# Strassen's scheme for layer 1 of the last two of four batches, in a fused attention and MLP kernel

## The chip, the cores and the metric

One core of a Trainium2 chip runs the whole program. The metric is device time in microseconds of one execution; a run's time is compared as the median of several.

## The reference

For each of 4 batches and 8 heads (768 positions, 64 features) a query sees a local window (keys less than 16 positions away) and 24 block summaries (the maximum of each 32 keys, the mean of each 32 values, with log 32 added to the score). The heads' outputs are joined to x, 3072 tokens of 512 features, and go through two layers:

```python
    a = np.exp(scores_all)
    a = a / (np.sum(a, axis=-1, keepdims=True) + 1e-09)
    v_all = np.concatenate([v, v_sum], axis=2)
    return np.matmul(a, v_all).astype(np.float32)
...
    h = x @ w_in
    g = np.maximum(0.01 * h, h)
    return (g @ w_out).astype(np.float32)
```

w_in is 512 x 2048, w_out 2048 x 512, all in fp32.

## The kernel before

**Split operands.** Both layers run in fp32r. Each operand is kept as a high part (rounded to fp32r) and a low part (what is left, in fp32r too), and a product is three matmuls: high x high, high x low, low x high. The weights are loaded raw, one 512 KB load per feature tile and layer, and split by `weights` (lines 613 to 651): ScalarE makes the high part (line 641), VectorE the low one (line 644). The parts stay in `win_hi`, `win_lo`, `wout_hi` and `wout_lo` for the whole run.

**Chunks.** The tokens go in 8 chunks of 384 (`T`), two to a batch. Chunk c has its x in one of two buffers, as 4 blocks of 128 features (`xh`, `xl`). `mlp` (line 665) works a chunk in 16 feature tiles of 128. `m1` is 12 matmuls (4 blocks of features, three products, 384 columns, line 676) into one of two PSUM banks `h`. ScalarE applies the leaky ReLU twice, to fp32r (`ghi`, line 683) and to fp32 (`gs`, line 680), and VectorE takes the difference (`glo`, line 686). `m2` is 9 matmuls of 512 columns (lines 695 to 697): three token blocks, three products, added over all 16 feature tiles into the three banks a0, a1, a2. TensorE's order is m1 of tile f, m2 of f-1, m1 of f+1, and so on. At a chunk's end the three banks are emptied by ScalarE, VectorE, ScalarE (`fin`, lines 708 and 710) and stored.

**Attention.** A unit is two heads by 128 queries, 12 units to a chunk, 96 in all. From chunk 2 on they run in quads of four: a burst of scores, transposes and products with the values is put between two MLP stages on TensorE; VectorE and ScalarE do the softmax. The values' product of a quad is copied into `xh` (line 563) and its rest into `xl` (line 566).

**The order.** `Plan` gives every operation an engine, a cost and a due time (`prio`), and simulates the engines: each takes, of what is ready, the one due first. The kernel is written out in the order that comes out, engine by engine; at run time each engine keeps to it and waits on semaphores. Due times are in units: one unit is an attention unit's share of a chunk, a chunk is 12 units, and the MLP begins at `LEAD` = 15.54. `PLACE` maps the attention units of a chunk to due times. Buffers are rings: an operation that allocates the k-th use of a tag waits for all users of the use before it. All loads and stores are issued by SyncE, in one queue. Raw weights, keys and block values share six buffers of 512 KB, `big`.

Of the kernel before, what the change touches and what calls it, by code (L numbers as in the profile page):

```python
# [8 lines left out]
F32 = mybir.dt.float32  # L9
# [28 lines left out]
PARTS = [(0, 0, SPL), (1, 0, NF), (0, SPL, NF)] + [(c, 0, NF) for c in range(2, NCH)]  # L38
XB = [0, 1] + [(c + 1) % 2 for c in range(2, NCH)]
PLACE = {0: (0.0, 1.0), 1: (13.07, 0.61), 2: (22.42, 0.495), 3: (36.92, 0.51)}  # L40
# [11 lines left out]
B1 = 6  # L52
USQ = 1.424
# [9 lines left out]
class Plan:  # L63
# [5 lines left out]
    def __init__(self):  # L69
        self.ops, self.rings, self.users = [], {}, {}  # L70
# [11 lines left out]
    def join(self, o, prio, after=(), use=(), alloc=()):  # L82
# [4 lines left out]
        for key in use:  # L87
            self.users.setdefault(key, []).append(o)

# [61 lines left out]
def build(tc, ctx, a):  # L151
# [5 lines left out]
    ps_acc, ps_h, ps_s, ps_t = psum("pacc", 1), psum("ph", 2), psum("pss", 1), psum("pst", 1)  # L157

    win_hi = cst.tile([128, 4, DF], F32R, name="win_hi")
    win_lo = cst.tile([128, 4, DF], F32R, name="win_lo")  # L160
# [10 lines left out]
    for i, (x, n) in enumerate(((xh, XGAP[0]), (xh, XGAP[1]), (xl, XGAP[2]), (xl, XGAP[3]))):  # L171
        gap(n, cst, f"x{i}")
        x.append(cst.tile([128, NP, T], F32R, name=f"x{i}"))
# [14 lines left out]

    mask_op = load_op(("mask",), -8.7, lambda: nc.sync.dma_start(out=mask, in_=a["mask"]), size=128 * (3 * LK + 44) * 4)
# [10 lines left out]
    def k_max(b, p, t, ahead):  # L200
        def load():
            x = new("big", ("kn", b * CPB, p), [128, 1024], bufs=BIG)
# [6 lines left out]
        kn_op[key] = load_op(key, t - 1.3 - ahead, load, after=gate(b), alloc=[("big", key, BIG)], size=128 * (S + 2 * WIN) * 4)  # L209
# [4 lines left out]
    def v_mean(b, j, t, ahead):  # L214
        def load():
            x = new("big", ("vb", b, j), [128, 1024], bufs=BIG)
# [10 lines left out]
        o = load_op(("vb", b, j), t - 1.0 - ahead, load, after=gate(b), alloc=[("big", ("vb", b, j), BIG)], size=96 * 4096)  # L227
# [6 lines left out]
    def v_mean_pe(t):  # L234
        def load(j):
            x = new("big", ("vb", 0, j), [128, 1024], bufs=BIG)
# [13 lines left out]
        for j in range(3):  # L250
            o = load_op(("vb", 0, j), t - 4.5 + 0.1 * j, lambda j=j: load(j), alloc=[("big", ("vb", 0, j), BIG)], size=128 * 4096)
# [6 lines left out]
    def operands(c, p, t, ahead):  # L258
# [5 lines left out]
        def load_k():  # L264
            x = new("big", kw, [128, 1024], bufs=BIG)
# [26 lines left out]
        if cb:  # L292
            kn_op[kw] = load_op(kw, t - 1.3 - ahead, load_k, alloc=[("big", kw, BIG)], size=128 * (T + 2 * WIN) * 4)
# [61 lines left out]
    def x_of(x, c, r, n):  # L355
        return x[XB[c]].rearrange("p a t -> p (a t)")[:, 128 * r:128 * r + n]
# [485 lines left out]
```

## Time and profile before

| | |
|---|---|
| median of 3 runs | 640.75 us (640.72 to 641.19) |
| span of the profiled execution, first to last instruction | 639.2 us |
| matmuls | 4592 |
| TensorE, busy | 633.7 us (99%) |
| VectorE, busy | 263.4 us (41%) |
| ScalarE, busy | 293.2 us (46%) |
| moved by DMA | 58.07 MB, mean 91 GB/s |
| granted TensorE clock, mean | 0.999 of 2.4 GHz |

The profiled execution has no time of its own beside its span; the runs' median is 1.55 us more than that. Matmuls overlap, so the time that one costs is the distance between two starts and not its duration.

### The profile page before, as it was taken

The numbers are of one execution on the slowest core, as the hardware profiler recorded it, in microseconds if no ns is written. First come the engines' busy times: TensorE is split into PE (matmuls) and PEld (weight loads), VectorE is DVE, ScalarE is ACT, GpSimd is POOL, SyncE is SP. The second block draws the span as 40 slices with busy tenths as digits, with TensorE's granted clock in tenths as the row PEclk, the third lists the DMA queues.
The fourth block names the chain that finished last, engine by engine and source line by source line (L and its number), as shares of the span: only waits on it lengthen the run. The fifth ranks groups of instructions, "written<-read, shape, count | busy, mean of one in ns | idle before, by whom it ended". The sixth has DMA issues, their size and how long they took to land.

```text
span 639.2 us, 11599 instructions
## 1 busy us (share of the span) xinstructions
PE 633.7 (99%) x4592; PEld 557.6 (87%) x4592; DVE 263.4 (41%) x881; ACT 293.2 (46%) x876; POOL 4.4 (1%) x10
## 2 busy tenths in 40 slices
PE   9999999999999999999999999999999999999997
PEld 7688888898888998888888888888898898989996
DVE  5899999512485213323533243132332422121111
ACT  5899985624655224435345254243543532222221
POOL 0200000000000000000000000000000000000000
PEclk9999999999999999999999999999999999999999
DMA  8897997200754100304332121111101200010001
GB/s 272 275 303 240 295 296 219 75 4 26 199 157 126 40 2 14 122 24 125 87 86 72 42 68 33 47 63 32 41 13 47 86 1 1 1 50 0 1 1 50
DMA packets 27206, 58.07 MB, mean 91 GB/s; under 512 B 3024, under 2 KB 13328, under 8 KB 27152
## 3 DMA queue, kind: packets, MB, share of 16 engines
q1 hardware_dynamic: 27152, 57.33, 29.3%
q8 instruction: 36, 0.59, 0.4%
q14 instruction: 18, 0.15, 0.1%
HBM read 48.97 MB, written 6.29 MB: 86 GB/s over the span
## 4 chain that ended last, share of the span: by engine, by line
PE 99%; ACT 0%; issue 0%; DVE 0%
PE h L676 42%; PE a L695 14%; PE a L697 14%; PE a L696 14%; PE spare L788 2%; PE vps L243 1%; PE t L346 1%; PE o L352 1%; PE s L329 1%; PE s_('B', 21)_5358 L352 0%; PE s_('B', 8)_2162 L352 0%; PE s_('B', 24)_6023 L352 0%; PE s_('B', 23)_5837 L352 0%; PE s_('B', 20)_5118 L352 0%; PE s_('B', 19)_4871 L352 0%; PE s_('B', 18)_4629 L352 0%
## 5 line engine op out<-in xcount | busy, mean ns | idle before, releaser
L676 PE MATMUL h<-x,win_hi 128*128 128x384 f32 x1024 | 262.8, 337 | 0.0
L686 DVE TENSOR_TENSOR glo<-gs,ghi 128x384 fp32r<-128x384 f32 x128 | 71.3, 557 | 304.5 <-ACT gs L680 304.2
L676 PEld LDWEIGHTS h<-x,win_hi 128*128 128x128 f32 x1024 | 185.8, 188 | 9.1 <-issue 0.2
L683 ACT ACTIVATE ghi<-h 128x384 fp32r<-128x384 f32 x128 | 62.8, 490 | 279.1 <-PE h L676 279.1
L676 PE MATMUL h<-x,win_lo 128*128 128x384 f32 x512 | 172.2, 336 | 0.0
L695 PE MATMUL a<-wout_hi,ghi 128*128 128x512 f32 x384 | 153.2, 399 | 0.0
L697 PE MATMUL a<-wout_hi,glo 128*128 128x512 f32 x384 | 151.1, 394 | 0.0
L696 PE MATMUL a<-wout_lo,ghi 128*128 128x512 f32 x384 | 150.2, 391 | 0.0
L676 PEld LDWEIGHTS h<-x,win_lo 128*128 128x128 f32 x512 | 96.1, 188 | 0.0
L697 PEld LDWEIGHTS a<-wout_hi,glo 128*128 128x128 f32 x384 | 72.1, 188 | 16.9 <-DVE glo L686 0.3
L696 PEld LDWEIGHTS a<-wout_lo,ghi 128*128 128x128 f32 x384 | 72.2, 188 | 11.3 <-DVE wout_lo L644 0.3
L695 PEld LDWEIGHTS a<-wout_hi,ghi 128*128 128x128 f32 x384 | 72.2, 188 | 10.5
L341 ACT ACTIVATE e<-e,m 128x120 f32<-128x120 f32 x192 | 73.4, 387 | 3.5 <-DVE m L334 3.5
L680 ACT ACTIVATE gs<-h 128x384 f32<-128x384 f32 x128 | 62.2, 486 | 0.0
L341 ACT ACTIVATION_READ_ACCUMULATOR e<-e,m 128x1 f32 x192 | 36.6, 191 | 0.0
L274 ACT COPY k<-kn 128x288 f32<-128x288 f32 x64 | 24.5, 432 | 5.9 <-DMA kn<-in_k_dram 5.9
L583 DVE TENSOR_TENSOR e<-e,z 128x480 f32<-128x480 f32 x36 | 23.6, 657 | 1.0
L638 DVE SCALAR_TENSOR_TENSOR raw<-raw 128x512 int32<-128x512 int32 x32 | 21.7, 689 | 0.7 <-ACT raw L635 0.3
L635 ACT ACTIVATE raw<-raw 128x512 f32<-128x512 f32 x32 | 21.4, 696 | 0.1
L207 DVE TENSOR_REDUCE ksum<-kn 128x24 f32<-128x768 f32 x16 | 15.1, 946 | 9.6 <-DMA kn<-in_k_dram 9.6
L334 DVE DVE_READ_ACCUMULATOR2_ANT m<- 128x1 f32 x192 | 15.9, 83 | 0.0
L223 DVE TENSOR_REDUCE vsum<-vb 96x32 f32<-96x1024 f32 x12 | 14.4, 1206 | 2.1 <-DMA vb<-in_vb_dram 2.1
(410 smaller groups left out, 455.8 us busy)
## 6 DMA issues: line engine op xcount, KB each, us to landing
raw<-in_w_dram SPq DMA_DIRECT2D x32, 512.0 KB
v<-in_v_dram SPq DMA_DIRECT2D x32, 288.0 KB
kn<-in_k_dram SPq DMA_DIRECT2D x16, 400.0 KB
k<-in_q_dram SPq DMA_DIRECT2D x32, 192.0 KB
out_dram<-out SPq DMA_DIRECT2D x21, 256.0 KB
vb<-in_vb_dram SPq DMA_DIRECT2D x12, 384.0 KB
kn<-in_k_dram SPq DMA_DIRECT2D x16, 208.0 KB
v<-vsum SPq DMA_DIRECT2D x24, 72.0 KB
```

The lines of the kernel that those rows point to most:

```text
L274: nc.scalar.copy(k, x)
L341: nc.scalar.activation(out=e[:, n], in_=e[:, n], func=AF.Exp, scale=-1.0, bias=m[:, n:n + 1], accum_out=z[:, n:n + 1])
L583: nc.vector.tensor_tensor(out=e, in0=e, in1=z.unsqueeze(2).broadcast_to([128, 4, LK]), op=ALU.mult)
L635: nc.scalar.activation(out=hw(), in_=hw(), func=AF.Prelu, scale=2.0 ** -112, alpha=2.0 ** 32)
L638: nc.vector.scalar_tensor_tensor(out=li(), in0=hi_i(), scalar=3, in1=li(), op0=ALU.logical_shift_left, op1=ALU.bitwise_or)
L676: nc.tensor.matmul(h[:, :T], w[:, k, 128 * f:128 * f + 128], x[:, k], start=n == 0, stop=n == 11)
L680: nc.scalar.activation(out=new("gs", G("gs", f), [128, T], bufs=1), in_=tl[G("h", f)][:, :T], func=AF.Prelu, alpha=0.01)
L683: nc.scalar.activation(out=gnew("ghi", G("ghi", f)), in_=tl[G("h", f)][:, :T], func=AF.Prelu, alpha=0.01)
L686: nc.vector.tensor_tensor(out=gnew("glo", G("glo", f)), in0=tl[G("gs", f)], in1=tl[G("ghi", f)].bitcast(F32), op=ALU.subtract)
L695: nc.tensor.matmul(o, gh, wout_hi[:, f], start=f == f0, stop=False)
L696: nc.tensor.matmul(o, gh, wout_lo[:, f], start=False, stop=False)
L697: nc.tensor.matmul(o, gl, wout_hi[:, f], start=False, stop=f == f1 - 1)
```

## The change

Chunks 0 to 3 stay as they were. For batches 2 and 3 both chunks of a batch go through layer 1 together:

- x of the batch is seen as four blocks: features in two halves, tokens in two halves (the two chunks). w_in of a pair of feature tiles is seen as four blocks too: features in two halves, the two tiles. Seven products of sums of blocks take the place of eight products (Winograd's form of Strassen's scheme). Each product is 6 matmuls of 384 columns: two 128-feature blocks, three parts.
- `prepare` (once per pair of tiles, in chunks 1 and 2) makes four weight sums and splits them, and writes these and the three plain blocks that are needed to HBM: 7 x 256 KB per pair, by six DMAs. Both batches read them back, product by product, into a ring of eight slots, six of them in a former x buffer.
- `take` copies attention's output of batches 2 and 3 to fp32 pieces in the old `big` slots 3 to 5, and `convert` makes the sums of x and splits them into the space of `win_hi` and `win_lo` (the last one in the other former x buffer).
- `product` runs the seven products of a pair on four banks: X for 1 and 2, Y for 6, W for 7 and 4, Z for 5 and 3. VectorE adds what crosses between banks (U2, U3, C22, C21, C12). The results go through the leaky ReLU and the split into `g`.
- Layer 2 comes after each two pairs (`GF` = 4 feature tiles): for each of six blocks of 128 tokens two halves of 6 matmuls into one bank, h1 or a0, and `flush` adds the bank to a sum in SBUF. The last group's blocks are stored one by one.
- `big` is six buffers until due time 23.1 and then three. Attention of chunks 3 to 5 is due earlier.

The core of the diff:

```diff
-PARTS = [(0, 0, SPL), (1, 0, NF), (0, SPL, NF)] + [(c, 0, NF) for c in range(2, NCH)]
-PLACE = {0: (0.0, 1.0), 1: (13.07, 0.61), 2: (22.42, 0.495), 3: (36.92, 0.51)}
+PARTS = [(0, 0, SPL), (1, 0, NF), (0, SPL, NF), (2, 0, NF), (3, 0, NF)]
+PLACE = {0: (0.0, 1.0), 1: (13.07, 0.61), 2: (22.42, 0.495), 3: (33, 0.8), 4: (43.2, 0.6), 5: (50.4, 0.7)}
+PLACE.update({c: (59.84 + UPC * (c - 6), 1.0) for c in range(6, NCH)})
+LATE = 23.1
+RS = 8
+GF = 4
+L1W = 2.8
+AHEAD = 2.5
...
+    NJ = NF // 2
+    ORDER = ("1", "6", "7", "5", "2", "4", "3")
+    PIECES = ((0, 1), (1, 2), (3, 4), (4, 5))
...
+        wa = w_op[2 * j, 0] + w_op[2 * j + 1, 0] + w_op[NF - 1, 1]
...
+                ks[n, l] = P.op("SP", 550, t + 0.02 * (2 * n + l), lambda n=n, w=w, l=l: keep(w, n, l), after=wa, size=128 * (2 - n) * 1024)
+        o = fw = P.op("DVE", DVE(1024), t, lambda: nc.vector.tensor_tensor(out=F, in0=win_hi[:, own].bitcast(F32), in1=win_lo[:, own].bitcast(F32), op=ALU.add),
...
+        for n, x in enumerate(((3, 2, 3, ALU.add), (2, 0, 2, ALU.subtract), (0, 3, 0, ALU.subtract), (1, 1, 0, ALU.subtract))):
+            o = P.op("DVE", DVE(256), t + 0.05 + 0.01 * n, lambda x=x: mix(*x), after=[o], use=[kf])
+        h = P.op("ACT", ACT(1024), t + 0.1, lambda: nc.scalar.copy(hi, F), after=[o], use=[kf], alloc=[("big4", kh, 1)])
...
+        c1 = split("1", full(0))
+        t3 = [mix(2, 3, 2, ALU.subtract, full(2, 3))]
+        t2 = [mix(0, 2, 0, ALU.add, t3 + c1)]
+        c6 = split("6", t2)
+        c7 = split("7", t3)
+        t4 = [mix(2, 1, 0, ALU.subtract, full(1) + t2 + c7)]
+        t1 = [mix(0, 3, 0, ALU.subtract, c6 + t4)]
+        split("5", t1)
+        split("2", full(1))
+        split("4", t4)
+        split("3", full(3))
...
+                for k in range(2):
+                    for l, y in ((0, 0), (0, 1), (1, 0)):
+                        nc.tensor.matmul(o[:, :T], w[:, 256 * l + 128 * k:256 * l + 128 * k + 128], x[y][:, T * k:T * k + T],
+                                         start=start and n == 0, stop=n == 5, skip_group_check=True)
...
+                    elif q == "6":
+                        u2 = [add("U2", "Y", "P1", True, d, [o] + c1)]
+                    elif q == "7":
+                        u3 = [add("U3", "W", "U2", True, d, [o] + u2)]
+                        hold["W"] = [o] + u3
+                    elif q == "5":
+                        c22 = [add("U3", "Z", "U3", False, d, [o] + u3)]
+                        hold["Z"] = [o] + c22
+                        gate_out(2 * j + 1, 1, "U3", c22, d + 0.6)
+                    elif q == "2":
+                        gate_out(2 * j, 0, "X", [o], d + 0.1)
+                    elif q == "4":
+                        c21 = [add("P1", "W", "U2", False, d, [o] + u3)]
+                        gate_out(2 * j + 1, 0, "P1", c21, d + 0.1)
+                    elif q == "3":
+                        c12 = [add("U2", "Z", "U2", False, d, [o] + c22 + c21)]
+                        gate_out(2 * j, 1, "U2", c12, d + 0.3)
...
+            parts = [(0, 0, 0), (0, 1, 0), (0, 0, 1), (0, 1, 1), (0, 2, 0), (0, 2, 1)] + [(1, i, s) for i in range(TPC) for s in range(2)]
...
+                    for f in (GF * n + 2 * s, GF * n + 2 * s + 1):
+                        gh, gl = (y[:, 128 * i:128 * i + 128] for y in g_of(f, h))
+                        for g, w in ((gh, wout_hi), (gh, wout_lo), (gl, wout_hi)):
+                            nc.tensor.matmul(o, g, w[:, f], start=s + m == 0, stop=s == 1 and m == 5)
...
+    for j in range(NF // 2):
+        prepare(j, LEAD + 14 + 2.2 * j)
+    for b in range(SB, B):
+        convert(b, LEAD + 24 * b - 3.2)
+        strassen(b, LEAD + 24 * b)
```

## Rows read from the trace of the kernel before

**Rows 1.** Page, part 1: busy time, share of the span, instructions.

```profile
span 639.2 us, 11599 instructions
PE 633.7 (99%) x4592; PEld 557.6 (87%) x4592; DVE 263.4 (41%) x881; ACT 293.2 (46%) x876; POOL 4.4 (1%) x10
```

**Rows 2.** Page, part 4: the chain that ended last, by engine and line.

```profile
PE 99%; ACT 0%; issue 0%; DVE 0%
PE h L676 42%; PE a L695 14%; PE a L697 14%; PE a L696 14%; PE spare L788 2%; PE vps L243 1%; PE t L346 1%; PE o L352 1%; PE s L329 1%; PE s_('B', 21)_5358 L352 0%; PE s_('B', 8)_2162 L352 0%; PE s_('B', 24)_6023 L352 0%; PE s_('B', 23)_5837 L352 0%; PE s_('B', 20)_5118 L352 0%; PE s_('B', 19)_4871 L352 0%; PE s_('B', 18)_4629 L352 0%
```

**Rows 3.** Windows of five stretches: length, busy PE, PEld, DVE, ACT, POOL, clock, DMA share, GB/s.

```profile
50.00:80.00 30.00, 29.97 (x247) 25.82 (x246) 29.29 (x85) 28.63 (x77) 0.00 (x0) 1.00 0.86 272
80.00:120.00 40.00, 40.00 (x271) 35.31 (x270) 35.54 (x82) 27.58 (x67) 0.00 (x0) 1.00 0.71 216
160.00:200.00 40.00, 40.00 (x343) 35.15 (x341) 24.41 (x75) 20.96 (x68) 0.00 (x0) 1.00 0.63 179
480.00:520.00 40.00, 40.00 (x286) 35.62 (x285) 10.89 (x35) 14.88 (x42) 0.00 (x0) 1.00 0.18 53
560.00:600.00 40.00, 40.00 (x202) 36.17 (x202) 6.56 (x12) 9.37 (x21) 0.00 (x0) 1.00 0.06 20
```

**Rows 4.** Timeline of TensorE, 622 to 631 us: start, duration, instruction.

```profile
622.10 0.33 PE L676 MATMUL h<-x,win_lo 128*128 128x384 f32 x1
622.27 0.39 PE L695 MATMUL a<-wout_hi,ghi 128*128 128x512 f32 x1
...
624.34 0.51 PE L676 MATMUL h<-x,win_hi 128*128 128x384 f32 x2
...
626.41 0.39 PE L695 MATMUL a<-wout_hi,ghi 128*128 128x512 f32 x1
...
628.49 0.51 PE L676 MATMUL h<-x,win_hi 128*128 128x384 f32 x2
...
630.59 0.39 PE L695 MATMUL a<-wout_hi,ghi 128*128 128x512 f32 x1
```

**Rows 5.** Timeline of TensorE just after an attention burst.

```profile
559.74 0.51 PE L695 MATMUL a<-wout_hi,ghi 128*128 128x512 f32 x1
560.08 0.40 PE L696 MATMUL a<-wout_lo,ghi 128*128 128x512 f32 x1
```

**Rows 6.** Groups of instructions: busy us, mean ns, idle before.

```profile
L686 DVE TENSOR_TENSOR glo<-gs,ghi 128x384 fp32r<-128x384 f32 x128 | 71.3, 557 | 304.5 <-ACT gs L680 304.2
...
L683 ACT ACTIVATE ghi<-h 128x384 fp32r<-128x384 f32 x128 | 62.8, 490 | 279.1 <-PE h L676 279.1
...
L680 ACT ACTIVATE gs<-h 128x384 f32<-128x384 f32 x128 | 62.2, 486 | 0.0
...
L223 DVE TENSOR_REDUCE vsum<-vb 96x32 f32<-96x1024 f32 x12 | 14.4, 1206 | 2.1 <-DMA vb<-in_vb_dram 2.1
...
L644 DVE TENSOR_TENSOR win_lo<-raw,win_hi 128x512 fp32r<-128x512 f32 x16 | 11.1, 696 | 0.9 <-ACT win_hi L641 0.7
L641 ACT CAST win_hi<-raw 128x512 fp32r<-128x512 f32 x16 | 10.9, 681 | 1.5 <-DVE raw L638 1.3
...
L708 DVE COPY out<-a 128x512 f32<-128x512 f32 x7 | 4.8, 691 | 2.0 <-PE a L697 2.0
...
L386 DVE TENSOR_TENSOR e<-e,z 128x240 f32<-128x240 f32 x12 | 4.7, 402 | 0.1
```

**Rows 7.** Timeline of the end, SPq being SyncE's DMA queue.

```profile
634.15 1.71 SPq L713 DMA_DIRECT2D out_dram<-out  x3
...
634.48 0.40 PE L697 MATMUL a<-wout_hi,glo 128*128 128x512 f32 x1
634.92 0.58 ACT L710 COPY out<-a 128x512 f32<-128x512 f32 x1 [0.79 <-PE a L697]
```

**Rows 8.** Page, parts 2 and 6: GB/s in 40 slices; DMA issues.

```profile
GB/s 272 275 303 240 295 296 219 75 4 26 199 157 126 40 2 14 122 24 125 87 86 72 42 68 33 47 63 32 41 13 47 86 1 1 1 50 0 1 1 50
...
raw<-in_w_dram SPq DMA_DIRECT2D x32, 512.0 KB
...
out_dram<-out SPq DMA_DIRECT2D x21, 256.0 KB
```

More of the change, by code (lines that the diff above doesn't have):

```diff
@@ L88, in join, with settle @@
             self.users.setdefault(key, []).append(o)
+    def settle(self, tag, choose):
+        insts = sorted(self.rings.pop((tag, 0)), key=lambda x: x[:2])
+        last = {}
+        for n, x in enumerate(insts):
+            place = min(choose(x[0]), key=lambda p: last.get(p, -1))
+            last[place] = n
+            self.slot[x[2]] = place
+            self.rings.setdefault((place, 1), []).append(x)
     def order(self):
@@ L172, in build @@
         gap(n, cst, f"x{i}")
-        x.append(cst.tile([128, NP, T], F32R, name=f"x{i}"))
+        x.append(cst.tile([128, NP * T], F32R, name=f"x{i}", tag=f"x{i}"))
+    big = cst.tile([128, BIG * 1024], F32, name="big")
+    raw = big[:, 3072:]
+    scratch = ctx.enter_context(tc.tile_pool(name="hbm", bufs=1, space=bass.MemoryType.DRAM))
+    sums = scratch.tile([NF // 2, 7, 128, 512], F32, name="sums")
     make_identity(nc, ident)
@@ L187, in new, with bigs, bank @@
         return tl[key]
+    def bigs(key):
+        n = int(P.slot[key][3:])
+        tl[key] = big[:, 1024 * n:1024 * n + 1024]
+        return tl[key]
+    def bank(key, tag=None):
+        tag = tag or P.slot[key]
+        return new(tag, key, [128, 512], src=ps_h if tag[0] == "h" else ps_acc, bufs=1)
     mask_op = load_op(("mask",), -8.7, lambda: nc.sync.dma_start(out=mask, in_=a["mask"]), size=128 * (3 * LK + 44) * 4)
@@ L370, in qk @@
                 if wide:
-                    new("h", K(f"s{h}"), [128, 512], src=ps_h)
+                    bank(K(f"s{h}"))
                 else:
@@ L560, in av, with take @@
                 values(u, tl["s0", kb1], 128 * n)
+        piece = 3 * (c % CPB) + r // 4
+        kx = ("R", c // CPB, piece)
+        def take():
+            nc.scalar.copy(raw[:, 512 * piece:512 * piece + 512], tl["s0", kb1])
         def xhi():
@@ L671, in m1 @@
         def m1(f, ks):
[L672 removed]
+            h = tl[G("h", f)] if ks[0] else bank(G("h", f))
             n = 3 * ks[0]
@@ new lines, in build, with convert, mix, split @@
+    conv_op = {}
+    def convert(b, t):
+        R = lambda *ns: [("R", b, p) for p in sorted({p for n in ns for p in PIECES[n]})]
+        full = lambda *ns: [x_op["R", b][p] for p in sorted({p for n in ns for p in PIECES[n]})]
+        step = [0]
+        def mix(o, x, y, op, after):
+            step[0] += 1
+            return P.op("DVE", DVE(768), t + 0.15 * step[0], lambda: nc.vector.tensor_tensor(out=half(o), in0=half(x), in1=half(y), op=op), after=after, use=R(o, x, y))
+        def split(q, after):
+            step[0] += 1
+            n, pos, key = OPER[q], ORDER.index(q), ("xc", b, ORDER.index(q))
+            hi, lo = xc(pos)
+            o = P.op("ACT", ACT(768), t + 0.15 * step[0], lambda: nc.scalar.copy(hi, half(n)), after=after, use=R(n), alloc=[(f"xc{pos}", key, 1)])
+            l = P.op("DVE", DVE(768), t + 0.15 * step[0] + 0.02, lambda: nc.vector.tensor_tensor(out=lo, in0=half(n), in1=hi.bitcast(F32), op=ALU.subtract), after=[o], use=R(n) + [key])
+            conv_op[b, pos] = [o, l]
+            return [o, l]
+        c1 = split("1", full(0))
[9 more added lines that the diff above has]
+        split("3", full(3))
```

268 lines of the change are left out of this document (219 added, 49 removed).

## Prediction

> **What bounds the kernel now.** I read the busy shares first: in a span of 639.2 us TensorE is busy for 633.7 us [rows 1]. A busy TensorE need not be one that nothing can shorten, so next comes the chain that ended last: 99% of it lies on TensorE, 42% in line 676 (layer 1) and three times 14% in lines 695 to 697 (layer 2) [rows 2]. The stretches then say whether some stage differs [rows 3]: TensorE is at 40.00 of 40 us at the full clock (2.4 GHz) in nearly all of them, also from 80 to 120 us, where VectorE has 35.54 of 40. From 560 to 600 us, where attention is over, VectorE needs 6.56 and ScalarE 9.37 of 40. So the time is the number of matmuls times their spacing, and the other engines have room, most of it late in the run, where the change puts its new work.
>
> The spacing is read from starts, since the durations overlap. Two feature tiles near the end [rows 4]: layer 1 runs from 624.34 to 626.41 and from 628.49 to 630.59, 12 matmuls in 2.07 and 2.10 us, so 2.085 / 12 = 173.8 ns; layer 2 from 622.27 to 624.34 and 626.41 to 628.49, 9 in 2.07 and 2.08 us, so 230.6 ns.
>
> The median of the runs, 640.75 us, is 1.55 us above the profiled span, for what lies around it; I take that remainder as unchanged and subtract from 640.75.
>
> **Layer 1 of batches 2 and 3.** Before: 2 chunks x 16 feature tiles x 12 = 384 matmuls per batch. After: 8 pairs of feature tiles x 7 products x 6 = 336, each again with 384 columns. So 48 fewer per batch, 96 in all: 96 x 173.8 ns = **16.7 us less**. If the new places of the operands (conversions in the old weight tiles, weights in the old x tiles) shift the spacing as much as the two tiles above differ, 172.5 to 175.0 ns, the 672 product matmuls move by 0.8 us either way.
>
> By the Trainium skill (TensorE: Matmul & The Clock Gate, Back-to-back issue gap) the gap is the columns over 2.4 GHz plus 2.5 ns, 162.5 ns for 384, and the gain would then be 15.6 us by estimate; the rows have 173.8 ns, and the rows are used.
>
> **Layer 2 in groups of four.** Before 2 x 16 x 9 = 288 matmuls per batch, after 4 groups x 6 blocks x 2 halves x 6 = 288, all 512 wide: nothing, within 0.3 us either way by the spacings above. What grows is the emptying of the accumulators: 24 per batch in place of 6. That is VectorE and ScalarE time, 18 x 0.69 us (L708) = 12 us per batch, spread over four groups [rows 6].
>
> More groups begin: for two batches 112 products and 192 half blocks, 304, in place of 128 (64 tiles, two stages). A new group costs nothing by itself: from layer 1 to layer 2 the step is 622.10 to 622.27, 0.17 us [rows 4]. It costs only after an attention burst, where the first step is 559.74 to 560.08, 0.34 us in place of 0.23 [rows 5]. The bursts stay as many, two per quad. I take 0.
>
> **Inside a group.** TensorE needs 14 products x 6 x 173.8 ns = 14.6 us, then 12 x 6 x 230.6 ns = 16.6 us, 31.2 us in all. For one pair of tiles (7.3 us) VectorE has five additions and four low parts, 9 x 0.56 = 5.0 us, and ScalarE nine passes, 9 x 0.49 = 4.4 us (L686, L683, L680) [rows 6]. Both fit. Latency counts more, since products 2, 4 and 3 accumulate onto banks that are read in the middle. The order 1, 6, 7, 5, 2, 4, 3 leaves room: product 7 ends its starts at 3.13 us after the pair's begin, its last matmul 0.17 us later (0.34 long), U3 takes 0.04 + 0.56 (the 0.04 from a matmul's end to the copy behind it, 634.88 to 634.92) [rows 6, 7], so it stands at 3.9 us, and product 4 begins at 5.2 us. Product 3 begins at 6.3 us and waits for C22, ready at 4.95 us. The next pair's product 1 needs bank X at 7.3 us; two ScalarE passes empty it by about 6.4 us. Least room: 0.9 to 1.3 us. The first half block that needs the second pair starts 2.8 us after the last product; its last operand goes through addition, two passes and a subtraction, 0.56 + 2 x 0.49 + 0.56 = 2.1 us after product 4, which ended 1.05 us earlier: room of 1.7 us.
>
> In batch 2's span attention of batch 3 shares both queues. From 480 to 520 us it adds 10.89 - 6.56 = 4.3 us to VectorE and 5.5 to ScalarE per 40 us [rows 3]; the 14.6 us of products then hold 10.0 + 1.6 = 11.6 us of VectorE. The longest instruction that can stand in an addition's way is the v sum, 1.21 us (L223) [rows 6], about the least room. I take 0.5 us of waiting for all eight groups; ends: 0, and one full v sum in every group of batch 2 and half of that in batch 3, 4 x 1.2 + 4 x 0.6 = 7 us.
>
> **Conversions.** Each batch has 11 VectorE passes over 768 columns and 7 of ScalarE. Lines 686 and 644 give (0.696 - 0.557) / 128 = 1.09 ns per column, so 0.97 us each [rows 6], 10.7 us; ScalarE 768 / 512 x 0.68 = 1.02 us at most (L641). They replace six low parts of 512 columns, 4.2 us, per batch. Cover at batch 2: its last attention piece is due at 61.9 in the planner's units, the tiles of chunk 3 run to 63.5, so some 2 layer-1 and 4 layer-2 stages, 12 us, remain on TensorE. At batch 3 the piece is due at 85.9 and layer 2 of the last group runs to 87.5: half of 16.6 us, 8.3 us. Product 1 needs early pieces only; product 6 needs two mixes and a split, about 5 us; product 5, three places on, some 10 us, and has 8.3 + 3.1 = 11.4 us. Close at batch 3, so 0.5 us; without the cover each batch would show its chain to product 5, about 10 us.
>
> **Weight sums.** Building them costs VectorE per pair 2 x 1.25 + 4 x 0.42 = 4.2 us (256 columns from L386), 33 us in all, in chunks 1 and 2. There VectorE has 24.41 of 40 us at the fullest stretch after the weights are split (160 to 200 us), and TensorE did not wait even at 29.29 of 30 (50 to 80 us) [rows 3]. I take 0. End: one VectorE pass of 1.25 us too late in each of eight pairs, but a tile's low part has some 2 us until its layer 2, so 0 to 2 us.
>
> They are written once, 14.7 MB, and read twice, 29.4 MB. Per group 14 loads of 256 KB, 3.7 MB in 31.2 us, are 118 GB/s; the page shows 272 to 303 GB/s where loads are dense [rows 8]. At 280 GB/s one load moves in 0.94 us against 1.04 us for its product, and eight slots are filled during layer 2. SyncE's queue gets 112 loads and 48 writes more; none waits for anything but a free slot or finished sums, and behind it stand the k, q and v loads of batch 3, wanted many us later. I take 0.
>
> The attention of batches 1 and 2 moves earlier and keeps its instructions: 0 on TensorE. The loads that share the big buffers get three slots in place of six from batch 1 on; what covers them is the distance to their layer 1, a chunk or more: 0, and one landing late would cost 2 us.
>
> **The end.** Now three stores follow the last matmul (634.48) within 1.4 us, and the last one's copy starts at 634.92 [rows 7]. After, the blocks end one by one and the last store is alone: gain 0 to 0.9 us (256 KB at 280 GB/s); the last emptying is VectorE's 0.69 in place of 0.58, 0.1 us more. I take 0.3 us less.
>
> **Sum.** 640.75 - 16.7 + 0.5 + 0.5 - 0.3 = **624.7 us**.
>
> **The rivals.**
> - *The conversion is not covered.* If the last attention piece comes after layer 2 of the group before, the chain to product 5, about 10 us, stands bare at one boundary or both: 634 or 644 us, and partly covered 628 to 634. For it: at batch 3 the room is 1.4 us by my count. Against: half of the chain hangs on early pieces.
> - *Slower: waits inside the pairs.* VectorE and ScalarE take instructions in order; if every pair of tiles waits, at the read of bank W before product 4, TensorE loses that wait 16 times. It decides from 16.7 / 16 = 1.04 us per pair; with a v sum's 1.21 us and an addition's 0.56 us in front, 1.8 us, it gives 640.75 - 17.0 + 16 x 1.8 = 652 us. For it: single banks, a chain over three engines. Against: 1.3 us of room each time, and attention is gone for batch 3.
> - *The weights from HBM come late.* If loads did not overlap and each took a fixed 2.6 us, 14 would need 36.4 us against 31.2, eight times 5.2: 665 us. The stretches with 272 to 303 GB/s of 512 KB loads speak against it [rows 8]. The Trainium skill (DMA: Bandwidth & Descriptors, Anatomy of one DMA) gives some 2 us plus bytes at 436 GB/s for one transfer, 2.6 us for 256 KB by estimate; by that rule, taken one after another, this rival would be the case.
> - *Group starts cost.* If each of the 304 groups paid what a start after a burst pays, 0.34 - 0.23 = 0.11 us, that would be 33 us; at half of it the gain is gone: 640 us. It is the case in which the change does not do what it says, fewer matmuls and no less time. The step between the stages speaks against it [rows 4].
>
> **How the numbers follow.** Chances: the forecast (621.5 to 628 us) 0.72; conversion bare 0.11, of which half stays below 634; waits in the pairs 0.08; late weights 0.04; group starts 0.05. Range: down by 0.8 + 0.3 + 0.6 of the end's bound and 1.0 of the waits, to 622.0; up to 631.0, which takes the upper parts of the waits (7 us) and half of the first rival. About 0.2% is what a measurement can tell from no change. Faster: 0.72 + 0.11 + parts of the others, 0.88; same 0.03; slower 0.09.
>
> **What would show it.** In the changed profile: 4,496 matmuls in place of 4,592; product starts 174 ns apart; TensorE 99% busy; no idle over 0.5 us in front of product 5 of a batch's first pair. Wrong would be idle TensorE behind the conversion's subtractions, behind an addition of a pair in batch 2, or behind loads of the sums, or product spacing above 180 ns.

## The result and the profile after

| | before | after |
|---|---|---|
| median of the runs | 640.74 us (640.50 to 641.19, 4 runs) | 624.73 us (623.69 to 626.83, 4 runs) |
| ratio, 95% interval | | 0.9757 [0.9739, 0.9776] |
| profiled execution: span | 639.2 us | 623.3 us (its own time: 625.08 us) |
| matmuls | 4592 | 4496 |
| VectorE, busy | 263.4 us (41%) | 367.1 us (59%) |
| ScalarE, busy | 293.2 us (46%) | 321.5 us (52%) |
| moved by DMA | 58.07 MB | 102.16 MB |

16.0 us less, and the terms of the prediction add up to 16.0. The same kernel, measured twice more beside other runs of the kernel before, gave 623.45 and 624.28 us (below).

The page of the changed kernel, parts 1 and 4, answers to [rows 1, 2].

```profile
span 623.3 us, 12015 instructions
PE 616.4 (99%) x4496; PEld 541.1 (87%) x4496; DVE 367.1 (59%) x1055; ACT 321.5 (52%) x914; POOL 4.4 (1%) x10
...
PE 94%; ACT 2%; DMA 2%; DVE 1%; issue 0%; DVEq 0%
PE L L989 21%; PE h L712 20%; PE a L731 7%; PE a L733 7%; PE a L732 7%; PE Z L899 5%; PE W L899 5%; PE X L899 5%; PE Y L899 3%; PE spare L1092 2%; DMA big<-in_w_dram 2%; PE vps L273 1%; ACT e L371 1%; PE s L359 0%; PE t L376 0%; ACT big L672 0%
```

TensorE still sets the time: 99% busy, 94% of the chain, and the 96 matmuls are gone. The other engines took on 104 us (VectorE) and 28 us (ScalarE) and 44 MB of transfers, and the chain shows nearly none of it: the 2% of the DMA line are loads of the raw weights at the start, not of the sums.

Four of the stretches of [rows 3], now in the changed kernel, with the same columns:

```profile
80.00:120.00 40.00, 40.00 (x244) 35.71 (x243) 39.34 (x88) 28.82 (x68) 0.00 (x0) 1.00 0.86 274
160.00:200.00 40.00, 40.00 (x372) 35.16 (x371) 35.85 (x112) 29.32 (x92) 0.00 (x0) 1.00 0.79 245
480.00:520.00 40.00, 40.00 (x223) 35.43 (x222) 21.97 (x34) 14.15 (x27) 0.00 (x0) 1.00 0.41 132
560.00:600.00 40.00, 40.00 (x209) 37.16 (x208) 18.78 (x35) 12.80 (x29) 0.00 (x0) 1.00 0.41 125
```

VectorE is at 39.34 of 40 us from 80 to 120 us and at 35.85 from 160 to 200 us, and TensorE still has 40.00 in both. Its waits, the whole list of the changed kernel (engine, line, releaser: us in total, times, longest):

```profile
PE spare L1092 <- DVE zero L1084: 1.0, 1, 1.0
PE a L732 <- DVE wout_lo L681: 0.5, 1, 0.5
PE a L731 <- ACT wout_hi L678: 0.2, 1, 0.2
```

None belongs to the new code: the first is the program's start, the other two are the first layer-2 tile at 49 us, which came before its raw weights had been split. Not one product or half block waits. (Two later executions have one more wait, at 118 us; see below.)

TensorE's timeline at the end of one group's products and through its layer 2 answers to [rows 4] (start, duration, instruction):

```profile
535.57 0.34 PE L899 MATMUL Z<-win_hi,x 128*128 128x384 f32 x1
...
536.61 0.34 PE L899 MATMUL X<-win_hi,x 128*128 128x384 f32 x1
...
537.65 0.34 PE L899 MATMUL W<-win_hi,x 128*128 128x384 f32 x1
...
538.70 1.21 PE L899 MATMUL Z<-x,x 128*128 128x384 f32 x6
539.75 0.39 PE L989 MATMUL L<-wout_hi,win_hi 128*128 128x512 f32 x1
...
541.60 0.39 PE L989 MATMUL L<-wout_hi,win_lo 128*128 128x512 f32 x1
...
544.32 0.39 PE L989 MATMUL L<-wout_hi,win_lo 128*128 128x512 f32 x1
```

A product takes 1.04 to 1.05 us, six matmuls 174 ns apart, whichever bank it goes to. Layer 2 has two paces: eight steps from 539.75 to 541.60 (231 ns each), then twelve to 544.32 (227 ns each). In [rows 4] nine steps took 2.07 and 2.08 us, 230.6 ns.

Of the new groups on the other engines (busy us, mean ns, idle before and its releaser), four are enough to check the durations that the prediction took from other rows:

```profile
L929 DVE TENSOR_TENSOR U<-Z,U 128x384 f32<-128x384 f32 x32 | 17.8, 555 | 6.0 <-PE Z L899 5.4
...
L869 DVE TENSOR_TENSOR win_lo<-big,win_hi 128x768 fp32r<-128x768 f32 x12 | 11.4, 953 | 0.3 <-ACT win_hi L868 0.3
L868 ACT CAST win_hi<-big 128x768 fp32r<-128x768 f32 x12 | 10.0, 836 | 4.1 <-DVE big L862 4.1
L826 DVE TENSOR_TENSOR big<-win_hi,win_lo 128x1024 f32<-128x1024 f32 x8 | 9.8, 1221 | 0.1
```

An addition that reads a PSUM bank takes 0.555 us (0.56 taken), a pass over 768 columns 0.95 us on VectorE (0.97) and 0.84 on ScalarE (1.02 at most), one over 1024 columns 1.22 us (1.25).

**Where 16 us came from.** I added up the distances between TensorE's starts by line over the last two batches. Before, 768 matmuls of layer 1 take 135.3 us; after, 672 of the products take 118.5: 16.8 us less, attention bursts included. Layer 2, in the stretches without a burst, goes from 229.7 to 227.6 ns a step, 576 x 2.1 ns = 1.2 us less. Against that stand 1.3 us in the first 60 us (1.2 of them for the late weights at 49 us) and 0.7 us more behind the last landing (1.4 us before, 2.1 after): 16.8 + 1.2 - 1.3 - 0.7 = 16.0, and the spans differ by 639.2 - 623.3 = 15.9 us.

### The profile page after: what moved, and what is told of

Same layout as the page of the kernel before. It is cut to its first block, busy times and chain, and to the rows that moved or that the text cites. A ratio compares the mean times of both kernels' runs of the same rounds, so it can differ in the third digit from the quotient of the medians.

```text
span 623.3 us, 12015 instructions
## 1 busy us (share of the span) xinstructions
PE 616.4 (99%) x4496; PEld 541.1 (87%) x4496; DVE 367.1 (59%) x1055; ACT 321.5 (52%) x914; POOL 4.4 (1%) x10
## 2 busy tenths in 40 slices
DMA packets 58443, 102.16 MB, mean 164 GB/s; under 512 B 5584, under 2 KB 30224, under 8 KB 58384
## 4 chain that ended last, share of the span: by engine, by line
PE 94%; ACT 2%; DMA 2%; DVE 1%; issue 0%; DVEq 0%
PE L L989 21%; PE h L712 20%; PE a L731 7%; PE a L733 7%; PE a L732 7%; PE Z L899 5%; PE W L899 5%; PE X L899 5%; PE Y L899 3%; PE spare L1092 2%; DMA big<-in_w_dram 2%; PE vps L273 1%; ACT e L371 1%; PE s L359 0%; PE t L376 0%; ACT big L672 0%
## 5 line engine op out<-in xcount | busy, mean ns | idle before, releaser
L712 PE MATMUL h<-x,win_hi 128*128 128x384 f32 x512 | 131.8, 338 | 0.0
L712 PEld LDWEIGHTS h<-x,win_hi 128*128 128x128 f32 x512 | 92.7, 188 | 4.1
L712 PE MATMUL h<-x,win_lo 128*128 128x384 f32 x256 | 86.1, 336 | 0.0
L731 PE MATMUL a<-wout_hi,ghi 128*128 128x512 f32 x192 | 77.4, 403 | 0.2 <-ACT wout_hi L678 0.2
L732 PE MATMUL a<-wout_lo,ghi 128*128 128x512 f32 x192 | 75.2, 392 | 0.5 <-DVE wout_lo L681 0.5
L733 PE MATMUL a<-wout_hi,glo 128*128 128x512 f32 x192 | 75.6, 394 | 0.0
L989 PE MATMUL L<-wout_hi,win_hi 128*128 128x512 f32 x192 | 75.2, 392 | 0.0
L989 PE MATMUL L<-wout_hi,win_lo 128*128 128x512 f32 x192 | 74.9, 390 | 0.0
L989 PE MATMUL L<-wout_lo,win_hi 128*128 128x512 f32 x192 | 74.8, 390 | 0.0
L712 PEld LDWEIGHTS h<-x,win_lo 128*128 128x128 f32 x256 | 48.0, 188 | 0.0
L940 ACT ACTIVATE win_hi<-U 128x384 fp32r<-128x384 f32 x32 | 16.6, 518 | 38.8 <-DVE U L929 38.8
```

The source lines that it names most:

```text
L712: nc.tensor.matmul(h[:, :T], w[:, 512 * f + 128 * k:512 * f + 128 * k + 128], x[:, T * k:T * k + T], start=n == 0, stop=n == 11)
L731: nc.tensor.matmul(o, gh, wout_hi[:, f], start=f == f0, stop=False)
L732: nc.tensor.matmul(o, gh, wout_lo[:, f], start=False, stop=False)
L733: nc.tensor.matmul(o, gl, wout_hi[:, f], start=False, stop=f == f1 - 1)
L940: nc.scalar.activation(out=hi, in_=ps("X") if direct else tl[kt], func=AF.Prelu, alpha=0.01)
L989: nc.tensor.matmul(o, g, w[:, f], start=s + m == 0, stop=s == 1 and m == 5)
```

## Experiments: is it the matmuls?

The theory: the gain is the 96 matmuls and nothing else moves; the rival: the new order also gives or takes something, and the sum only happens to agree. Three experiments tell them apart.

**Product 1 done twice.** The changed kernel, with product 1 of every pair issued twice into the same bank, so that layer 1 has as many matmuls as before, 4592:

```diff
-                n = 0
-                for k in range(2):
+                for _ in range(2 if q == "1" else 1):
+                    n = 0
+                    for k in range(2):
...
-            return P.op("PE", 6 * (T / 2.4 + 14.5), t, run,
+            return P.op("PE", (12 if q == "1" else 6) * (T / 2.4 + 14.5), t, run,
```

> Product 1 of each pair is computed twice (the second pass overwrites the first with the same values), so layer 1 of batches 2 and 3 has 384 matmuls per batch again and everything else stays as in the changed kernel. Theory (the gain is the 96 matmuls and nothing else): 96 x 174 ns = 16.7 us more, 641.4 us, a ratio to the kernel before of 1.000 to 1.003. Rival (part of the gain comes from the new layer 2, from better overlap or from the shorter tail): it stays 2 us or more below the kernel before, under 638.7 us. Rival (products wait for additions, and TensorE has idle time to give): the second pass fills the waits and costs less than 12 us, under 637 us.

Measured: 639.56 us (638.78 to 640.84, 10 runs) against 641.06 (21 runs of the kernel before), ratio 0.9976 [0.9967, 0.9985]; span 639.1 us. The products' starts, added up, grew by 16.7 us, from 118.5 to 135.2: 96 x 173.9 ns, what the sum had. But the whole is 1.5 us below the kernel before with as many matmuls, and the interval leaves out 1: so something else gives, too, and the expected 641.4 us were too many. Layer 2's pace, worked out above at 1.2 us, is most of it: its step is 227.7 ns in this kernel as well.

**One batch only.** Strassen's scheme for batch 3 alone, batch 2 as before (4544 matmuls):

```diff
-PARTS = [(0, 0, SPL), (1, 0, NF), (0, SPL, NF), (2, 0, NF), (3, 0, NF)]
-XB = (0, 1, 1, 0)
-SB = 2
+PARTS = [(0, 0, SPL), (1, 0, NF), (0, SPL, NF)] + [(c, 0, NF) for c in range(2, 6)]
+XB = (0, 1, 1, 0, 1, 0)
+SB = 3
```

> Only batch 3 goes through the seven products; batch 2 runs as two plain chunks. Theory: the gain is linear in the batches, 48 matmuls x 174 ns = 8.35 us, so 640.7 - 8.4 = 632.4 us, within 1.5 us. Rival (batch 2, beside which attention still runs, pays waits that batch 3 does not): more than half of the gain stays, under 630.5 us. Rival (the boundary into the last batch, with its late attention piece, costs time): less than half stays, over 634.5 us.

Measured: 632.04 us (631.49 to 632.18, 4 runs), ratio 0.9859 [0.9845, 0.9872], 9.0 us less. Half of 16.7 is 8.35, and half of layer 2's 1.2 makes it 8.95: both terms go by the batch.

**The changed kernel again**, twice, because its first profiled execution has the late weights at 49 us and its runs spread over 3 us:

> The changed kernel as it is, once more. In its first profile TensorE stood 1.2 us at about 49 us for a raw weight load that landed late, and the span ended 5.4 us after the last matmul's start in place of 4.7 us. If both are chance of the loads, this profile has the first smaller or elsewhere and the runs spread over 3 us as before (623.7 to 626.8); if they belong to the change, both stand again at the same places.

Measured: 623.45 us (623.04 to 624.11, 4 runs), ratio 0.9727 [0.9714, 0.9741]; profiled span 621.5 us. TensorE's list of waits in this execution:

```profile
PE spare L1092 <- DVE zero L1084: 1.0, 1, 1.0
PE to_('B', 6)_1731 L376 <- DVE z L615: 0.2, 1, 0.2
```

> The changed kernel as it is, for the other two kernels of this call to be held against on the same chip: 623.4 to 624.7 us. If the loads at the start are what spreads its runs, the profile again differs from the first one in the first 60 us and in the end alone, within 0.3 us from chunk 4 to the last matmul.

Measured: 624.28 us (623.72 to 624.63, 5 runs), ratio 0.9742 [0.9729, 0.9756]; span 622.3 us. Neither has the waits on wout_lo and wout_hi. Whether the first raw weights of layer 2 are split in time differs from one execution to the next, and is worth 1.2 us; up to there the loads are issued in the same order as in the kernel before. From the first product to the last matmul's start TensorE takes 268.09, 268.11 and 268.09 us in the three executions of the changed kernel, so what differs lies ahead of the products and behind the last matmul.

Ahead of them, both later executions have a wait that the first has not. In this one it is 0.4 us, and the page's line on its chain (part 4) follows:

```profile
PE to_('B', 6)_1731 L376 <- DVE z L615: 0.4, 1, 0.4
```

```profile
PE 86%; DVE 7%; ACT 4%; issue 1%; DMA 1%; DVEq 0%
```

At 118 us the transposes of an attention burst wait for the softmax on VectorE, which has just done an addition of the weight sums (L819, from 116.89 us). Between 100 and 130 us the two executions lose 0.4 and 0.6 us against the first, which ran 1.7 us behind them there, because of its start, and found the softmax done. The chain of both goes over VectorE and ScalarE ahead of that wait. So the fuller VectorE from 80 to 120 us is not quite free; which part of it the sums have, and which the attention that moved earlier, no run tells apart. The gain in these two measurements is 17.6 and 16.6 us; their profiled executions differ by 0.3 us up to the first product and by 0.5 us behind the last matmul's start.

## Experiments: why is layer 2's step shorter?

In the kernel before layer 2 comes in runs of 9 matmuls between two tiles' layer 1; after, in runs of 6 to 72, most of them 30 or longer. The theory: after a switch the first eight or so steps are longer, and longer runs have fewer of them. So I made the runs longer in the kernel before.

**Paired by due times.** In the last four chunks the due times of two tiles' layer 2 put next to each other:

```diff
+            tm = t + 1.5 * fs
+            if c >= 4:
+                tm, t = t + (2.5 - f % 2 * 0.9) * fs, t - f % 2 * 0.9 * fs
```

> The kernel before, with the stages of its last four chunks in pairs: layer 1 of two feature tiles, then layer 2 of two tiles; the same instructions. It asks for the spacing of layer 2, 229.7 ns on average before and 227.6 ns in the changed kernel (starts without a burst between). Theory (long runs of layer 2 keep a shorter spacing, the first steps after a switch are the slow ones): the mean falls by 0.7 to 1.5 ns and the time by 0.4 to 1.0 us. Rival (the operands' new places make the difference): mean and time as in the kernel before, 640.7 us within 0.3 us. If the layer 2 of a pair has to wait for its low part, TensorE shows idle time and it is slower.

Measured: 640.60 us (639.72 to 642.10, 11 runs), ratio 0.9998 [0.9989, 1.0007]. The trace shows why it says nothing: the planner kept runs of 9 and made a single run of 18. A due time is a wish, and the next kernel uses a dependence.

**Paired by force.** Layer 2 of an even tile waits for layer 1 three tiles on:

```diff
+            if c >= 4 and f % 2 and f >= f0 + 3:
+                m2_of[f - 3]["after"].append(o)
```

> The kernel before again, its last four chunks in true pairs: layer 2 of an even tile now waits for layer 1 of the tile three on, so that layer 2 comes 18 matmuls at a time where no burst lies between; the same instructions. (Without that wait the planner kept runs of 9.) Theory (after a switch to layer 2 the first eight steps take 231 ns, the later ones 226.6, whatever the operands): in a run of 18 the last ten steps are at 227, the mean of layer 2 in these chunks falls by 1.5 ns where runs of 18 stand, and the time by 0.3 to 0.9 us. Rival (the new places of the operands in the changed kernel are the cause): all steps stay near 229.7 and the time at 640.9.

Measured: 640.83 us (640.12 to 641.70, 11 runs) against 641.02 (15 runs), ratio 0.9993 [0.9981, 1.0004]. There are 23 runs of 18. TensorE's timeline in one of them:

```profile
592.36 0.39 PE L695 MATMUL a<-wout_hi,ghi 128*128 128x512 f32 x1
...
594.21 0.39 PE L697 MATMUL a<-wout_hi,glo 128*128 128x512 f32 x1
...
596.27 0.39 PE L697 MATMUL a<-wout_hi,glo 128*128 128x512 f32 x1
```

Eight steps of 231 ns up to 594.21, as after; the nine behind them take 2.06 us, 229 ns, not 227. The mean over all runs of 18 is 229.2 ns against 229.7 in runs of 9. So the length of a run explains 0.5 of the 2.1 ns, and the theory falls for the rest. The two kernels also differ in where `g` lies and in how many matmuls go to one bank in a row (6 or 12 against 3); neither was tried. In the last nine steps of a run of 18 the distances repeat in threes, 230.5, 227.5 and 228.6 ns on average; in the changed kernel they are 226.6 to 226.8 ns from the tenth step of a run on, also where the bank changes. The cause of the 227 ns stays open. It is 1.2 us of 16.

## Experiments: how much room had the pairs?

VectorE's U3 stands between product 7 and product 4, which overwrites bank W. In the changed kernel's timeline (DVE is VectorE):

```profile
527.20 0.34 PE L899 MATMUL W<-win_hi,x 128*128 128x384 f32 x1
...
528.44 0.56 DVE L929 TENSOR_TENSOR U<-W,U 128x384 f32<-128x384 f32 x1 [0.43 <-PE W L899]
...
530.33 0.34 PE L899 MATMUL W<-win_hi,x 128*128 128x384 f32 x1
```

Product 7 starts at 527.20, U3 ends at 529.00, product 4 starts at 530.33: 1.33 us of room. Read so in all 16 pairs, the room is 1.32 to 1.35 us in first pairs of a group, 1.17 to 1.21 in second pairs of batch 3, 2.6 to 2.7 in most second pairs of batch 2 (an attention burst lies between), 0.88 in the last pair of batch 2 and, least, 0.74 in the first pair of batch 3. To see whether that is what stands between this kernel and the rival that lost, U3 was made longer: the same addition done several times into the same place.

**Four times, the planner told.**

```diff
-                            nc.vector.tensor_tensor(out=o, in0=ps(s), in1=tl[K(y)], op=ALU.add)
-                        return P.op("DVE", DVE(T), prio, run,
+                            for _ in range(4 if first and out == "U3" else 1):
+                                nc.vector.tensor_tensor(out=o, in0=ps(s), in1=tl[K(y)], op=ALU.add)
+                        return P.op("DVE", DVE(T) * (4 if first and out == "U3" else 1), prio, run,
```

> The addition U3, which stands between product 7 and products 4 and 5's addition, is done four times over (the same result each time): 3 x 0.56 = 1.7 us more on VectorE in each of 16 pairs, 27 us in all. Theory (the chain inside a pair has about 1.3 us of room and no more): product 4 waits some 0.4 us per pair, 0.4 x 16 = 6 us, 628 to 632 us, with idle TensorE ahead of product 4. Rival 1 (VectorE is nowhere near the path): no change, within 1 us of 624. Rival 2 (VectorE's queue is already the pace in the pairs): each addition shows in full, 27 us, 650 us.

Measured: 626.43 us (625.02 to 627.52, 4 runs), ratio 0.9766 [0.9743, 0.9789]. Only three waits of bank W on U3, 1.2 us in all. The expectation missed: the planner, told of the longer addition, moved product 6 earlier in some pairs, and room was made where there was none. What the experiment showed is that the order adapts; the room itself it did not measure.

**Four times, the planner not told.** The same without the change of cost, so that TensorE's order is that of the changed kernel, instruction for instruction:

```diff
-                            nc.vector.tensor_tensor(out=o, in0=ps(s), in1=tl[K(y)], op=ALU.add)
+                            for _ in range(4 if first and out == "U3" else 1):
+                                nc.vector.tensor_tensor(out=o, in0=ps(s), in1=tl[K(y)], op=ALU.add)
```

> U3 four times over as in the kernel before this, but the planner is not told: every engine keeps the order of the changed kernel, and only 3 x 0.56 = 1.7 us of VectorE stand in each pair's chain. Theory (the room ahead of product 4 is 1.3 us): product 4 waits 0.4 us in each of 16 pairs, 6 us, 630 us, with idle TensorE ahead of product 4 in every pair; attention beside batch 2 adds to it. Rival (the chain has more room than I counted): under 626 us. Rival (VectorE's queue is the pace): 16 x 1.7 = 27 us, 651 us.

Measured: 636.51 us (635.75 to 637.17, 5 runs) against 640.90 (9 runs), ratio 0.9933 [0.9921, 0.9946]; span 634.6 us. The waits of TensorE that are not in the changed kernel:

```profile
PE W L899 <- DVE U L930: 7.9, 13, 1.3
PE L L990 <- DVE y L1013: 1.2, 1, 1.2
```

and one of them in the timeline:

```profile
510.61 0.34 PE L899 MATMUL W<-win_hi,x 128*128 128x384 f32 x1
...
510.83 0.55 DVE L947 TENSOR_TENSOR win_lo<-U,win_hi 128x384 fp32r<-128x384 f32 x1
...
511.48 2.33 DVE L930 TENSOR_TENSOR U<-W,U 128x384 f32<-128x384 f32 x4
...
512.70 0.33 PE L899 MATMUL X<-win_hi,x 128*128 128x384 f32 x1
...
513.86 0.45 PE L899 MATMUL W<-win_hi,x 128*128 128x384 f32 x1 [0.84 <-DVE U L930]
```

Two things are to be seen. First, the listed wait is less than the loss: from 512.70 to 513.86 are 1.16 us where 0.17 would do, 0.99 lost, and 0.84 listed, since the list counts from the end of a matmul and matmuls overlap. 13 waits of W cost 7.9 us by the list; with 0.17 us of lost overlap and 0.11 us of a slower next step each (0.28 in place of 0.17: 505.44 to 505.72 in another pair) 11.5 us, with y's 1.2 us 12.7. From start to start the trace has a little more: TensorE takes 281.7 us from the first product to the last matmul, 13.6 more than the changed kernel's 268.1, of which 11.4 stand at bank W and 1.7 in layer 2. The spans differ by only 634.6 - 622.3 = 12.3 us, mostly because this execution took 4.2 us behind its last matmul's start and the other 5.4. Second, a pair passes its delay on. The addition is 2.33 - 0.56 = 1.77 us longer. A first pair with 1.33 us of room should lose 0.44 and loses about 0.5 (0.05 us pass from U3's end, 513.81, to product 4's start, 513.86, even when it waits); a second pair with 1.2 should lose 0.57 and loses 1.0, because its product 7 had ended at 510.95 while VectorE still made a low part of the pair before (510.83 to 511.38), which was late itself. I had expected 630 us and missed by the second pairs and layer 2.

**Twice, the planner not told.** The same with `range(2 ...)`, 0.59 us more per pair, less than the least room of 0.74:

> The same with U3 twice over, 0.56 us more per pair, the planner not told. Theory (1.3 us of room): covered in every pair of batch 3 and in most of batch 2, 0 to 1 us, at most 625 us. Rival (waits in the pairs begin at once): 0.56 x 16 = 9 us, 633 us.

Measured: 623.45 us (622.41 to 624.89, 4 runs), ratio 0.9731 [0.9718, 0.9744]; TensorE never waits for U3, and from the first product to the last matmul it takes 268.3 us in place of 268.1. 0.59 us of additional VectorE work per pair is all but free, 1.77 us cost 13.6 / 16 = 0.85 us per pair: the edge that the rival needed is real, and lies between.

## Experiments: the two covers

**The last attention piece later.** The conversion of a batch needs the last of its attention pieces. The due times of chunk 7's attention were put 2 units later (24 units are a batch's four groups of 31.2 us, so some 10 us):

```diff
+PLACE[7] = (73.84, 1.0)
```

> The attention of batch 3's second chunk is due two units later (73.84 for 71.84), so that its last piece comes at the end of layer 2 of batch 2's last group and the conversion loses its 8 us of cover; the planner writes the order anew around it. Nothing is left out. Theory (the conversion is covered in the changed kernel, and its chain to product 5 is some 10 us with 3 us of products beside it): up to 7 us slower than the changed kernel's 623.5 to 624.7, 626 to 631 us, with TensorE idle at one place, just ahead of the first products of batch 3; what half blocks of layer 2 the planner holds back for that place comes off. Rival (the conversion hardly matters, since early pieces carry most of it): within 1 us of the changed kernel.

Measured: 629.08 us (628.19 to 629.45, 4 runs), ratio 0.9806 [0.9787, 0.9826]; some 5 us above the changed kernel. First the changed kernel at this boundary, rows of its timeline:

```profile
483.28 1.15 PE L382 MATMUL s_('B', 24)_5642<-pt,v 120*64 120x64 f32 x32
...
484.48 0.59 ACT L596 COPY big<-s_('B', 24)_5642 128x512 f32<-128x512 f32 x1 [5.64 <-PE s_('B', 24)_5642 L382]
...
485.10 0.96 DVE L862 TENSOR_TENSOR big<-big 128x768 f32<-128x768 f32 x1 [2.38 <-ACT big L596]
...
491.30 0.34 PE L899 MATMUL X<-win_hi,x 128*128 128x384 f32 x1
...
493.74 0.34 PE L899 MATMUL W<-win_hi,x 128*128 128x384 f32 x1
...
493.94 0.95 DVE L869 TENSOR_TENSOR win_lo<-big,win_hi 128x768 fp32r<-128x768 f32 x1
...
496.19 0.34 PE L899 MATMUL Y<-win_hi,x 128*128 128x384 f32 x1
```

The last piece is there at 485.07 (484.48 + 0.59), and the passes run from 485.10 to 494.89. But TensorE does not stand at batch 3's first product: between product 1 (X, 491.30), product 7 (W, 493.74) and product 6 (Y, 496.19) the planner laid half blocks of layer 2 of batch 2, and all of the passes are covered. With the piece later (its products with the values at 493.02) the half blocks are used up:

```profile
493.02 1.15 PE L383 MATMUL s_('B', 24)_5703<-pt,v 120*64 120x64 f32 x32
...
497.23 0.67 PE L900 MATMUL X<-win_hi,win_lo 128*128 128x384 f32 x1 [1.81 <-ACT C L944]
497.70 0.52 PE L900 MATMUL X<-win_lo 128*128 128x384 f32 x1
...
502.85 0.45 PE L900 MATMUL Y<-win_hi,x 128*128 128x384 f32 x1 [0.65 <-DVE U L930]
```

TensorE waits 1.81 us, later 0.65, and between them the steps are 0.32 us in place of 0.17. The planner had put products 1 and 2 of the first pair and product 1 of the second ahead of those that need the late piece; what the last of these waits for is bank X, which ScalarE empties in two passes (from 495.58 and 496.69 us, the second is L944) with a pass of the conversion between them. The stretches of the same kernel show the granted clock with it (the columns are those of [rows 3], the clock stands behind POOL):

```profile
490.00:495.00 5.00, 5.00 (x52) 4.27 (x52) 0.88 (x3) 1.23 (x3) 0.00 (x0) 1.00 0.46 147
495.00:500.00 5.00, 3.19 (x12) 2.87 (x11) 5.00 (x7) 3.47 (x6) 0.00 (x0) 0.73 0.24 83
500.00:505.00 5.00, 4.11 (x20) 3.47 (x19) 4.33 (x6) 1.68 (x3) 0.00 (x0) 0.93 0.57 157
```

So the bare part of the conversion costs its waits and, behind the first, nine steps at the lower level, 384 / 1.2 GHz = 0.32 us each: 9 x (0.32 - 0.17) = 1.3 us more.

**Four slots for the weights.** The ring that is read back from HBM with four slots for eight:

```diff
-RS = 8
+RS = 4
...
-        begin(f"r{n}", P.users["x", 2])
-    for n in (6, 7):
-        begin(f"r{n}", spans(4608, 512))
+        if n < RS:
+            begin(f"r{n}", P.users["x", 2])
```

> The ring for the weight sums has four slots in place of eight; loads and products stay the same. Theory (loads overlap and are fast, and eight slots are ample): a slot comes free 3.1 us before its next product, a load lands some 2.3 us after its issue at the soonest (the last store before took 635.5 to 637.8), so four slots are about enough and the time rises by 0 to 4 us, 624 to 628 us. Rival (late loads set the pace as soon as they cannot run far ahead): ten of 14 loads per group come 1 us late or more, eight groups, 80 us or more.

Measured: 627.82 us (627.39 to 629.41, 4 runs), ratio 0.9793 [0.9773, 0.9814]; 3 to 4 us above the changed kernel. TensorE's waits:

```profile
PE Z L899 <- DVE U L929: 1.0, 2, 0.8
PE o L382 <- POOL v L315: 1.0, 1, 1.0
...
PE X L899 <- DMA x<-sums: 0.5, 1, 0.5
```

Only one wait, of 0.5 us, is for a load of the sums; the others came with the order that the planner made for the smaller ring, and what of them hangs on SyncE's queue was not followed up. So even four slots, with 14 loads to a group, bring the weights nearly in time, and the rival of loads one after another, each with its fixed cost, is out. The trace of the changed kernel shows why: SyncE issues the loads of a pair 1.04 us apart (528.43, 529.47, 530.52 us), and counting the queue's packets off at 256 KB a load, each is through 2.3 to 2.9 us after its issue, so two or three are under way at once. The 2.6 us of the rival were about right for one load; what failed is that they follow one another. The section of the Trainium skill behind that figure (DMA: Bandwidth & Descriptors, Anatomy of one DMA) is on transfers that GpSimd issues; these are SyncE's, and the trace agrees with its size. In the stretch from 560 to 600 us of the changed kernel all transfers together are 125 GB/s, where the prediction had 118 for the sums. (The 272 to 303 GB/s that it set against this leave out one slice of 240 [rows 8]; nothing hung on it.)

## Why the prediction was right, step by step

The predicted time, 624.7 us, is the first median to 0.03 us, which is better than its steps were: four terms were off by 0.3 to 1.2 us, and with the chance of one execution's start they cancelled. That closeness is luck; what was right is the mechanism and the largest term.

- **Layer 1 of batches 2 and 3** (-16.7): right. The spacing of the products without bursts is 174.3 to 174.7 ns, by bank, against 173.8 from [rows 4] and the bounds of 172.5 to 175.0, and doubling product 1 gave 16.7 us back. By the formula of the Trainium skill (TensorE: Matmul & The Clock Gate, Back-to-back issue gap), which that section gives for an isolated matmul, 162.5 ns by estimate, the same 96 matmuls would have been 15.6 us; the trace does not agree with it, and the rows were the better price.
- **Layer 2 in groups of four** (0, within 0.3): wrong by 1.2 us. The term took 288 matmuls per batch at an unchanged spacing. The trace has 227.6 ns in place of 229.7. One part is shown (longer runs have fewer of the slow first steps), the larger is open. The group starts cost nothing, as taken: the step from a product to layer 2 in the timeline (six starts of Z and the step to 539.75 take 1.05 us together) is no longer than one between products. The prediction counted these groups wrong: 4 groups x 6 blocks x 2 halves are 48 half blocks per batch, so 96 and not 192 for both, and 208 groups and not 304. Its rival on group starts would have cost 208 x 0.11 = 23 us and not 33; it did not come about either way.
- **Inside a group** (+0.5): the room was right, the charge was not. Forecast were 1.3 us in front of product 4 and 0.9 as the least; read are 1.32 to 1.35 in first pairs and 0.74 as the least. The v sums, which the prediction feared most, were never in the way: the last one runs at 313 us, ahead of the first product at 349.8. With so much room TensorE waited 0.0 us. The rival that this step fed, waits in the pairs, is shown to be a matter of one microsecond: 0.59 us more per pair costs next to nothing, 1.77 us bring the time to 636.5.
- **Conversions** (+0.5): the passes were right (0.95 and 0.84 us), the cover was right in size and wrong in kind. I counted 11.4 us of layer 2 and early products against a chain of 10 us, in the order of the loops. The planner keeps half blocks back and puts them between the first products, so the charge was 0. The rival, a bare conversion, is real: a later piece costs 5 us.
- **Weight sums** (0): right in the first execution, short by 0.4 and 0.6 us in the two later ones. The work on VectorE is 8 x (2 x 1.22 + 4 x 0.42) = 33 us, as forecast, and it lies between 100 and 200 us. My fullest stretch was the wrong one: from 80 to 100 us VectorE splits raw weights and is at 19.79 of 20 us in both kernels; from 100 to 120 us it goes from 15.75 to 19.54, and 5.7 us of that are the first sums (lines 826, 819 and 831). So the sums and the attention that moved earlier filled VectorE to 98% of 40 us, which I had not foreseen. TensorE waited for none of it in this execution, where it was late itself, and once in each of the other two, at 118 us.
- **The end** (-0.3): not there. The last rows of TensorE and of its queue in the changed kernel's timeline are

```profile
617.69 1.69 SPq L1019 DMA_DIRECT2D out_dram<-rows  x2
617.90 0.39 PE L989 MATMUL L<-wout_hi,win_lo 128*128 128x512 f32 x1
```

  the last matmul starts at 617.90 and the last store has landed 3.29 us later; before, from 634.48 [rows 7], it was 3.28. The lone store is no faster than the last of three: over the executions with a profile it is 2.8 to 3.4 us in both kernels.
- **Around the span**: 1.55 us were taken as unchanged; it was 625.08 - 623.3 = 1.8. Not foreseen was the start: 1.3 us in the first profiled execution, none by 60 us in the two later ones.

Against a forecast of -16.0 stand -16.8 for layer 1, -1.2 for layer 2, 0 for the waits in the pairs, the conversions and the end, and what differs by the execution: 1.3 us at the start or 0.4 to 0.6 us at 118 us, and up to 0.7 us behind the last landing. The three measurements are -16.0, -17.6 and -16.6. The range of 622.0 to 631.0 holds all three.

## What to carry to other kernels

Where one engine is busy throughout and its instructions have a steady spacing, a change is worth the instructions it takes away times the distance of two starts, read from rows near the place; the rest of the work is to check that every new chain on the other engines is shorter than what TensorE has to do meanwhile, pair by pair and boundary by boundary. A busy share of 98% on a second engine over 40 us cost 0 to 0.6 us here, by the execution: it says little by itself. Latency between two uses of a bank can cost far more: measure that room in the trace, and lengthen the instruction in it to see where it ends. An experiment in a planned kernel should leave the planner's costs alone, or the order moves and a different kernel is measured.

## What the runs showed that was not expected

- Layer 2's matmuls of 512 columns are 231 ns apart in the first eight steps after a switch from 384 columns and 227 ns after that in the changed kernel; in the kernel before, forced into runs of 18, 231 and then 229 ns.
- After the wait of 1.81 us in the kernel with the late piece TensorE was granted the lower of its two levels for nine matmuls (0.32 us a step, granted clock 0.73 in that stretch of 5 us). Before the fall it had been at 5.00 of 5 us and then idle for 1.81 us. The waits of the kernel with four additions, up to 1.3 us, were followed by one step of 0.28 us, and its granted clock stayed at 0.999 over the whole span.
- A wait in the list is 0.15 to 0.17 us less than what it costs with matmuls of 384 columns, and the next step adds 0.11: 13 waits listed at 7.9 us cost about 11.5.
